# Attention and MLP mixer on one core: chunks of weights in the units' ring, and eight sums of weights moved into the first element's channel mixing

## The chip, the cores and the metric

The kernel runs on one core of a Trainium2 chip. The metric is the device time of one execution in microseconds (us). The core has five engines with a queue of instructions each, worked off in order: TensorE (PE; its weight loads are listed as PEld), VectorE (DVE), ScalarE (ACT), GpSimd (POOL) and the sync engine (SP), which here issues nearly all DMA transfers. An instruction that waits holds everything behind it in its queue. All data are float32, but the four weight matrices come as float64 and are converted to float32 by the kernel.

## The reference, cut to what matters

```python
# q, k, v: (8, 12, 448, 64); w_tok1 (448, 256), w_tok2 (256, 448), w_ch1 (768, 1536), w_ch2 (1536, 768)
q_n, k_n = rmsnorm(q, g_q), rmsnorm(k, g_k)
attn = softmax(q_n @ k_n.T / 8) @ v                  # per batch and head
x = attn.transpose(0, 2, 1, 3).reshape(8, 448, 768)
u = x + (relu(x.T @ w_tok1) @ w_tok2).T              # token mixing
out = u + relu(u @ w_ch1) @ w_ch2                    # channel mixing
```

## The kernel before, in words

**Batches.** The work goes over eight batches (elements) b, each with six pairs of head pairs in attention. Attention of batch b+1 runs beside the mixing of batch b: lists of small work items with a cost each are merged by `merge` in proportion to their costs, and `run` emits them in that order. This order is the order in which PE, DVE, ACT and POOL work; they are not reordered. The DMA issues of the sync queue are placed by a scheduler as they become ready in its own reckoning, so their order is seen in the built program.

**Mixing of one batch.** The attention result is held transposed, `uT` (768 rows in six tiles of 128, by 448). For token mixing it is turned: DVE transposes it into `xt` (L655, in the pool "tu", which has one buffer), four stores bring it to a DRAM scratch `xs` (L623), and a load brings it back as `x` (L630; the pool "x" has two buffers, one for each half). `tok1` (L669) and `tok2` (L677) are the two token products; DVE adds the second one to `uT` (L682). For batches 1 to 7 channel mixing uses seven products in place of eight (a Strassen form): the sums of activations go to "tu" (L698 to L701), `ch1` (L791) and `ch2` (L848) multiply by *units* of weights, 384 KB each, 42 per batch, which are loaded from a DRAM scratch `ws` by `load_units` (L724) into a ring of eight buffers (`unit_pool`). Four of the seven units of a group are plain blocks of the weights, or hold one; the rest are sums of the four blocks.

**Batch 0 prepares the weights.** Its channel mixing is done in the plain form, in 36 products of four matmuls each, one for every *chunk* of weights (`first_stage`, L765; L773 adds the second layer's result to `uT`). The 36 chunks (four blocks of 128 by 128, 512 KB in float64 and 256 KB in float32; w_ch1 is chunks 0 to 17, w_ch2 chunks 18 to 35) are loaded by two transfers each (`weight_load`, L177, five buffers in `raw_pool`), converted by bit operations (L248, L249, L251 and L266 on DVE, L259 on ACT) and written as a *stage* (L293 on DVE, `convert_last`), which PE multiplies by and which is also stored to `ws` (L193). Where a stage lies is told by `stage_home`: chunks 8 to 12 and 21, 22 in a tile of the pool "tu", chunks 13 and 14 in the pool "h1", the others in the ring of units, which no unit needs before batch 1. `weight_items` is the pipeline: item i loads chunk i+2, begins the conversion of chunk i, and ends that of chunk i-2. `first_items` places these items among the products: item k of the rest, which ends chunk 13+k, goes behind product `begins(k)`.

**Sums.** The seven-product form needs four sums of the four blocks of each chunk. `make` computes them on POOL in four instructions (L205 to L208), `send` stores them (L212). For the last six chunks (`direct`) they are made from the stage while it is still there. For the other 30 (`one`) the four blocks are loaded back from `ws` (L228) into a buffer of `raw_pool`, summed and stored; each of these steps lies one or more items behind the one before. The first three of these items run in the tail of batch 0, the next 25 in batch 1's token mixing and L791 part, the last five beside batch 1's L848 part. A unit that holds a sum can't be loaded before the sums of its group of chunks are sent (`has`): groups 0, 1, 2 are chunks 0 to 5, 6 to 11, 12 to 17; group 3 is 18 to 23, group 4 is 24 to 35.

**Output.** DVE turns each of the six output tiles of a batch (`trans_y`, L884, four buffers in `turn_pool`) and four stores send it (L613). The first four tiles of batch b are turned in the tail of batch b and sent in the token mixing of batch b+1; the last two are turned there, in buffers that the first two must have left.

Of the kernel before, what the change touches and what calls it, by code (L numbers as in the profile page):

```python
# [8 lines left out]
F32 = mybir.dt.float32  # L9
# [13 lines left out]
NQ = 8  # L23
# [21 lines left out]
def whole(ctx, tc, shifted, pre, q, k, v, g_q, g_k, moe_w_tok1, moe_w_tok2, moe_w_ch1, moe_w_ch2, out):  # L45


    nc = tc.nc
# [149 lines left out]
    def sum_items():  # L198
# [11 lines left out]
        def send(i):  # L210
            st["summed"].add(i)
            nc.sync.dma_start(out=slots(i, 4, 8), in_=eight(st.pop(("sum", i)))[:, 4:8])  # L212

        def direct(i):

            if i < n:
                st["sum", i] = raw_tile()
                make(st["stage", i], eight(st["sum", i]))
            if i > n - 6:
                send(i - 1)  # L220


        order = [*range(n - 18), *range(n - 12, n - 6), *range(n - 18, n - 12)]

        def one(i):
            if i < len(order):
# [7 lines left out]
                load_units(st["at"])  # L234

        def eight(t):
            return t[:].rearrange("p n w -> p (n w)").bitcast(F32).rearrange("p (q n) -> p q n", q=NQ)
        return ([(1.0, lambda i=i: direct(i)) for i in range(n - 6, n + 1)],
                [(1.0, lambda i=i: one(i)) for i in range(len(order) + 3)])

    def convert_first(i):
# [27 lines left out]
    def stage_home(j):  # L269


        if j in (8, 21):
            st["stages"] = tu_pool.tile([P, 4, KC, HS], F32, name="stages", tag="tu")
        if 8 <= j < 13 or 21 <= j < 23:
            o = (j - 8) % 13 * 4 * P
            return st["stages"][:].rearrange("p a b n -> p (a b n)")[:, o:o + 4 * P]
        if 13 <= j < 15:
            return h1_pool.tile([P, C], F32, name="stage", tag="h1")[:, 0:4 * P]
        t = unit_pool.tile([P, 3, 2, P], F32, name="stage", tag="unit")
        return t[:].rearrange("p t i n -> p (t i n)")[:, 0:4 * P]  # L280
# [351 lines left out]
            in_=st.pop("xs")[:].rearrange("(g p) n -> p g n", p=R))  # L632

    def x_tile(b, half):
        st["x", b, half] = x_pool.tile([P, KC, NS, P], F32, name="x")
        return st["x", b, half]

    def trans_x(b, j):
# [284 lines left out]

        return b < B - 1 and not shifted

    def first_items(tok, prods):


        convert = weight_items(BEFORE, len(chunks) + 3)
        items = merge(tok, convert[:5])  # L930
        n = len(stages) - 13
        for j, it in enumerate(prods[:-6]):
            items.append(it)
            items += [(0.0, convert[5 + k][1]) for k in range(len(convert) - 5) if begins(k, n) == j]
        return items, prods[-6:]

    def begins(k, n):

        return 2 + -(-k * 27 // (n - 1)) if k < n else 29

    def last_items(b):

# [45 lines left out]
    for part in pre.roots(2, st):  # L988
# [5 lines left out]

    run(merge(
        att_items(0, 8) + merge(att_items(8, AHEAD * per + 1), x_items(0, 0)), weight_items(0, BEFORE)))
    left, (direct, sums) = [], sum_items()
    for b in range(B):
        early, double = middle_items(b)
        if b == 0:  # L1000
            early, last = first_items(x_items(0, 1) + tok1_items(0, 0) + tok1_items(0, 1) + early, double)
        else:
            if in_next(b - 1):

                y, z = sends(b - 1, y_order(b - 1)[:4]), left
                left = [y[0], y[1], z[0], y[2], z[1], y[3]]
            run(merge(tok1_items(b, 0), left[:2]))
            begin, early = merge(tok1_items(b, 1) + early[:3 * KC], left[2:]), early[3 * KC:]
            if b == 1:
                early, double = merge(begin + early, sums[3:28]), merge(double, sums[28:])  # L1010
                begin = []
            early = begin + early + double
            early, last = early[:-4], early[-4:]
# [3 lines left out]
            att = att_items(lo, lo + 10) + x_items(b + AHEAD, 0) + att_items(lo + 10, lo + per)  # L1017
        if b == 0:
            last = x_items(1, 1) + merge(
                last, direct + sums[:3], turns(b, y_order(b)[:4], not in_next(b)))  # L1020
        else:
            if b + 1 < B:
                last = merge(last, x_items(b + 1, 1))
# [258 lines left out]
```

## Time and profile before

Median of 3 runs: 1362.38 us (1361.84 to 1365.18). The profiled execution: span 1360.3 us.

| engine | busy us | share | instructions |
|---|---|---|---|
| PE | 1290.7 | 95% | 7408 |
| PEld | 929.5 | 68% | 7408 |
| DVE | 748.0 | 55% | 1295 |
| ACT | 365.4 | 27% | 734 |
| POOL | 375.4 | 28% | 443 |

The stretches of the batches, cut at the first L669 of each:

| stretch, us | length | PE busy | POOL busy | DMA share |
|---|---|---|---|---|
| 92.60 to 272.70 (batch 0) | 180.10 | 172.33 | 32.45 | 0.60 |
| 272.70 to 452.45 (batch 1) | 179.75 | 163.66 | 102.58 | 0.93 |
| 452.45 to 610.00 (batch 2) | 157.55 | 154.70 | 40.01 | 0.67 |
| 610.00 to 767.60 (batch 3) | 157.60 | 154.73 | 40.03 | 0.68 |

How to read the views: a timeline line has the start and the length of a run of equal instructions, the engine, the line of the kernel, the operation with its output and inputs, and in brackets the idle time of the engine just before and what ended it. A busy PE is not a PE at full rate: after a stop its matmuls take longer. The DMA share is the mean busy share of the core's 16 DMA engines. The chain of work that ended last gives PE 78% of the span, DVE 10%, DMA 5%.

### The profile page before, as it was taken

Reading aid. Unit: us, or ns where it says so; the run is one execution under the profiler, and the core shown is the slowest. Engines: PE = TensorE matmul, PEld = TensorE weight load, DVE = VectorE, ACT = ScalarE, POOL = GpSimd, SP = SyncE. Lnnn points to the kernel's source line nnn. Section 1 sums busy time; section 2 is a strip of 40 time slices with the busy share of each in tenths; the row PEclk is TensorE's granted clock in tenths of the full one; section 3 lists DMA queues with packets and bytes.
Section 4 is the critical chain, followed back from the end, with each engine's and each line's share of the span. In section 5 each row is a group of like instructions: output and inputs, shape, how many; then the busy total and the mean of one; then the engine's idle time right before and its main releaser. Section 6 shows DMA issues by size and latency. Waiting matters only on the chain.

```text
span 1360.3 us, 20152 instructions
## 1 busy us (share of the span) xinstructions
PE 1290.7 (95%) x7408; PEld 929.5 (68%) x7408; DVE 748.0 (55%) x1295; ACT 365.4 (27%) x734; POOL 375.4 (28%) x443
## 2 busy tenths in 40 slices
PE   5989997998988999999999999999999999999997
PEld 3444443446777667794778757795777967787996
DVE  6878698563653366545556265644656365543212
ACT  5553442122320232303341123302322023300100
POOL 1211210366772231312231123312323133311220
PEclk9999998998999999999999999999999999999999
DMA  9655387689999666595568854595665956476654
GB/s 209 163 167 134 99 224 172 141 206 234 281 231 219 152 161 150 128 252 104 143 157 173 197 128 129 137 236 114 172 155 127 247 108 166 120 177 136 184 169 96
DMA packets 501520, 227.82 MB, mean 167 GB/s; under 512 B 373604, under 2 KB 463076, under 8 KB 501412
## 3 DMA queue, kind: packets, MB, share of 16 engines
q1 hardware_dynamic: 488290, 224.60, 67.1%
q10 hardware_dynamic: 12994, 1.84, 0.8%
q8 instruction: 61, 1.00, 0.3%
q14 instruction: 47, 0.39, 0.1%
q0 software_dynamic: 128, 0.00, 0.0%
HBM read 186.84 MB, written 39.52 MB: 166 GB/s over the span
## 4 chain that ended last, share of the span: by engine, by line
PE 78%; DVE 10%; DMA 5%; ACT 2%; issue 2%; SPq 1%; POOL 1%; DVEq 0%; ACTq 0%; POOLq 0%
PE m_ps L848 24%; PE m_ps L791 19%; PE m_ps L765 8%; PE o_ps L443 8%; PE s_ps L369 7%; PE m_ps L669 6%; PE m_ps L677 3%; DVE es L411 2%; DVE qk_t L334 2%; DMA unit<-ws 2%; PE d_ps L423 1%; DMA v<-in_v_dram 1%; ACT e L373 1%; PE m_ps L423 1%; DVE qkT L349 1%
## 5 line engine op out<-in xcount | busy, mean ns | idle before, releaser
L848 PE MATMUL m_ps<-hb,unit 128*128 128x224 f32 x1764 | 341.5, 355 | 7.7 <-DMA unit<-ws 5.8
L848 PEld LDWEIGHTS m_ps<-hb,unit 128*128 128x128 f32 x1764 | 333.2, 191 | 22.6 <-issue 13.0
L791 PE MATMUL m_ps<-tu,unit 128*128 128x224 f32 x1008 | 204.4, 358 | 3.0 <-DVE r L796 3.0
L791 PEld LDWEIGHTS m_ps<-tu,unit 128*128 128x128 f32 x1008 | 190.1, 192 | 22.4 <-DVE r L796 5.1
L373 ACT ACTIVATE e<-s_ps 128x448 f32<-128x448 f32 x336 | 157.0, 548 | 105.5 <-PE s_ps L369 104.8
L791 PE MATMUL m_ps<-uT,unit 128*128 128x224 f32 x756 | 154.7, 357 | 5.6 <-ACT r L812 3.1
L443 PE MATMUL o_ps<-e,v 64*64 64x448 f32 x1316 | 153.7, 543 | 4.6 <-DMA v<-in_v_dram 4.5
L791 PEld LDWEIGHTS m_ps<-uT,unit 128*128 128x128 f32 x756 | 140.6, 190 | 21.9 <-DVE uT L682 6.0
L369 PE MATMUL s_ps<-qkT 64*64 64x448 f32 x1260 | 145.7, 547 | 1.4 <-ACT qkT L352 1.4
L857 POOL TENSOR_TENSOR uT<-uT,r 128x448 f32<-128x448 f32 (+1 forms) x56 | 51.9, 937 | 265.1 <-DVE r L857 148.7
L796 DVE TENSOR_TENSOR r<-m_ps,r 128x448 f32<-128x448 f32 x63 | 38.9, 618 | 122.4 <-PE m_ps L791 69.8
L443 PEld LDWEIGHTS o_ps<-e,v 64*64 64x64 f32 x1316 | 50.6, 133 | 76.8 <-issue 70.7
L411 DVE TENSOR_TENSOR es<-es,e 128x896 f32<-128x896 f32 x84 | 94.2, 1122 | 14.9 <-ACT e L373 11.7
L857 DVE TENSOR_TENSOR uT<-uT,m_ps 128x448 f32<-128x448 f32 (+1 forms) x70 | 34.0, 502 | 122.5 <-PE m_ps L848 122.5
L369 PEld LDWEIGHTS s_ps<-qkT 64*64 64x64 f32 x1260 | 44.1, 132 | 71.7 <-issue 60.3
L411 POOL TENSOR_TENSOR es<-e 128x896 f32<-128x896 f32 x21 | 43.9, 2088 | 160.1 <-ACT e L373 160.1
L796 POOL TENSOR_TENSOR hb<-r,r 128x448 f32<-128x448 f32 x21 | 27.9, 1326 | 216.1 <-ACT r L812 166.8
L669 PE MATMUL m_ps<-x,w_sb 112*128 112x384 f32 x256 | 87.2, 494 | 0.0
L677 PE MATMUL m_ps<-w_sb,h 128*128 128x448 f32 x192 | 77.8, 549 | 6.3 <-DVE uT L682 6.3
L352 ACT ACTIVATE qkT<-qkT,g_t 128x448 f32<-128x448 f32 x36 | 24.1, 668 | 216.2 <-DVE qkT L349 216.2
L1164 DVE TENSOR_REDUCE ms<-sq 128x28 f32<-128x896 f32 (+2 forms) x45 | 48.8, 1084 | 59.5 <-ACT sq L1150 56.7
L669 PEld LDWEIGHTS m_ps<-x,w_sb 112*128 112x128 f32 x256 | 48.6, 193 | 36.4 <-ACT e L373 4.2
(114 smaller groups left out, 1357.3 us busy)
## 6 DMA issues: line engine op xcount, KB each, us to landing
unit<-ws SPq DMA_DIRECT2D x294, 384.0 KB, 4.1
raw<-in_moe_w_ch_dram SPq DMA_DIRECT2D x72, 256.0 KB, 3.5
v<-in_v_dram SPq DMA_DIRECT2D x94, 112.0 KB, 4.2
xs<-xt SPq DMA_DIRECT2D x56, 168.0 KB, 4.5
x<-xs SPq DMA_DIRECT2D x14, 672.0 KB, 7.3
out_dram<-turned SPq DMA_DIRECT2D x168, 56.0 KB, 2.0
ws<-raw SPq DMA_DIRECT2D x36, 256.0 KB, 4.4
qk_t<-in_q_dram SPq DMA_DIRECT2D x144, 56.0 KB, 3.0
```

Of the source, the lines that this page charges most:

```text
L369: nc.tensor.matmul(out=pss[i][rows_of(i, a), 0:S], lhsT=qkT[h, 1, k * D:(k + 1) * D], rhs=qkT[h, 0, :], start=True, stop=True)
L373: nc.scalar.activation(out=e[:, i, :], in_=pss[i][:, 0:S], func=AF.Exp)
L411: eng.tensor_tensor(out=es[:], in0=(es if k > 1 else st["e", t, 0])[:], in1=st["e", t, k][:], op=ALU.add)
L443: nc.tensor.matmul(out=st["o", p][a * D:(a + 1) * D, 0:S], lhsT=vt[rows, k * D:(k + 1) * D], rhs=e[rows, :], **kw)
L669: nc.tensor.matmul(out=ps[:, 0:HC], lhsT=w1_sb[0:R, c, jc * P:(jc + 1) * P], rhs=st["x", b, h][0:R, :, c, :], start=(c == 0), stop=(c == N ...
L677: nc.tensor.matmul(out=ps[:, 0:S], lhsT=st["h1", jc][:, cc * P:(cc + 1) * P], rhs=w2_sb[:, jc].rearrange("p c r -> p (c r)"), start=(jc == ...
L765: nc.tensor.matmul(out=ps, lhsT=a[:, o + 2 * half, :], rhs=natural(half)[:, :, t, :] if wide else u[:, half * KC + t, :], start=(t == 0 an ...
L791: nc.tensor.matmul(out=ps[:, j * HS:(j + 1) * HS], lhsT=w[:, t, j, :], rhs=m, start=(t == 0), stop=(t == KC - 1))
L796: add = lambda e, o, x, y: e.tensor_tensor(out=o, in0=x, in1=y, op=ALU.add)
L848: nc.tensor.matmul(out=ps[:, j * HS:(j + 1) * HS], lhsT=st["w"](j, t), rhs=hb[:, HB[what], t, :], start=(t == 0), stop=(t == KF - 1))
L857: add = lambda e, o, x, y: e.tensor_tensor(out=o, in0=x, in1=y, op=ALU.add)
L1164: self.nc.vector.tensor_reduce(out=st["ms", p][:, p % 2, lo:hi], in_=sq[:, lo:hi], axis=AX_X, op=ALU.add)
```

## The change

It has three parts. (1) `stage_home`: chunks 21 and 22 no longer lie in a tile of "tu" but in the ring of units like their neighbours. (2) `begins`: the places of the conversions among the products of batch 0 become 2, 4, 5, 7, 8, 9, 11, 12, 14, 15 and then 17 to 29 one by one, instead of 27 products divided evenly, so that a chunk takes a place of the ring after the chunk eight before it is used. (3) `sum_items`: the sums of chunks 0 to 7 are taken out of the list that runs in batch 1 and become ten items `some`, placed behind every second product of batch 0's channel mixing. They use tiles named `few` in the two buffers of the pool "x", which are free between batch 0's `tok1` and the load of batch 1's first half of `x`. The list `sums` is then 25 items instead of 33; five of them run in the tail of batch 0, fifteen in batch 1's token mixing and L791 part, five beside its L848 part. The purpose is to take transfers and POOL work from batch 1 into batch 0, and to take the wait for "tu" away.

```diff
+        FEW = 8
+
+        def some(i):
+            if 2 <= i:
+                send(i - 2)
+            if i < FEW:
+                t = st["sum", i] = x_pool.tile([P, KC, NS, P], F32, name="few", tag="x")
+                nc.sync.dma_start(out=eight(t)[:, 0:4], in_=slots(i, 0, 4))
+            if 1 <= i <= FEW:
+                q = eight(st["sum", i - 1])
+                make(q, q)
...
-        order = [*range(n - 18), *range(n - 12, n - 6), *range(n - 18, n - 12)]
+        order = [*range(FEW, n - 18), *range(n - 12, n - 6), *range(n - 18, n - 12)]
...
-        return ([(1.0, lambda i=i: direct(i)) for i in range(n - 6, n + 1)],
+        return ([(0.0, lambda i=i: some(i)) for i in range(FEW + 2)],
+                [(1.0, lambda i=i: direct(i)) for i in range(n - 6, n + 1)],
                 [(1.0, lambda i=i: one(i)) for i in range(len(order) + 3)])
...
-        if j in (8, 21):
+        if j == 8:
             st["stages"] = tu_pool.tile([P, 4, KC, HS], F32, name="stages", tag="tu")
-        if 8 <= j < 13 or 21 <= j < 23:
-            o = (j - 8) % 13 * 4 * P
+        if 8 <= j < 13:
+            o = (j - 8) * 4 * P
...
-            items += [(0.0, convert[5 + k][1]) for k in range(len(convert) - 5) if begins(k, n) == j]
+            items += [(0.0, convert[5 + k][1]) for k in range(len(convert) - 5) if begins(k) == j]
+            if j % 2 and j < 2 * len(some):
+                items.append(some[j // 2])
...
-    def begins(k, n):
-
-        return 2 + -(-k * 27 // (n - 1)) if k < n else 29
+    def begins(k):
+
+
+        return 2 + -(-k * 14 // 10) if k < 10 else min(k + 7, 29)
...
-                early, double = merge(begin + early, sums[3:28]), merge(double, sums[28:])
+                early, double = merge(begin + early, sums[5:20]), merge(double, sums[20:])
...
-                last, direct + sums[:3], turns(b, y_order(b)[:4], not in_next(b)))
+                last, direct + sums[:5], turns(b, y_order(b)[:4], not in_next(b)))
```

## The prediction

> **What bounds the kernel now.** I read the page first: TensorE (PE) is busy for 1290.7 of 1360.3 us, so only stretches in which PE stands can be won. The second view is the busy time of every engine per stretch; I cut it where the batch's first token matmul (L669) starts. The pieces of batch 1 and of batch 2 (token mixing; seven-product part L791; part L848) stand below one another.
>
> ```profile
> core 0: us, PE busy (x) PEld busy (x) DVE busy (x) ACT busy (x) POOL busy (x), PEclk, DMA share, GB/s
> 272.70:303.25 30.55, 28.69 (x146) 13.23 (x145) 17.87 (x31) 9.74 (x22) 20.53 (x30) 1.00 0.86 204
> 303.25:389.62 86.37, 77.91 (x461) 57.05 (x459) 40.81 (x69) 24.64 (x51) 59.80 (x95) 0.96 0.98 255
> 402.50:452.45 49.95, 44.18 (x237) 40.55 (x236) 18.64 (x33) 4.22 (x8) 13.50 (x20) 0.97 0.95 220
> 452.45:482.10 29.65, 28.70 (x145) 13.07 (x143) 15.20 (x31) 9.56 (x22) 7.49 (x6) 1.00 0.51 104
> 482.10:555.40 73.30, 71.40 (x461) 54.33 (x460) 41.41 (x74) 25.75 (x54) 23.04 (x18) 1.00 0.63 160
> 555.40:610.00 54.60, 54.60 (x321) 49.96 (x318) 28.98 (x49) 6.46 (x12) 9.48 (x10) 1.00 0.81 195
> ```
>
> Batch 1 does the same matmuls as batch 2 and takes 179.75 us against 157.55: 30.55, 86.37 and 62.83 us (389.62 to 452.45) against 29.65, 73.30 and 54.60. Its DMA share of 0.98 in the L791 part says why: the sums of the weights are read and written back there. The same view gives batch 0 180.10 us (92.6 to 272.7), with one hole. The timelines of VectorE (DVE) and PE show it:
>
> ```profile
> 217.28 0.64 DVE L349 STREAM_TRANSPOSE qkT<-qk_t 128x448 f32<-128x448 f32 x1
> 221.06 1.70 DVE L655 STREAM_TRANSPOSE xt<-uT 128x448 f32<-128x448 f32 x3 [3.14 <-PE m_ps L765]
> ...
> 230.55 1.15 DVE L773 TENSOR_TENSOR uT<-uT,m_ps 128x448 f32<-128x448 f32 x2
> ```
> ```profile
> 231.22 8.06 PE L765 MATMUL m_ps<-hb,stage 128*128 128x448 f32 x16 [7.19 <-DVE uT L773]
> ```
>
> DVE waits 3.14 us for the one "tu" place, held by chunks 21 and 22 until PE has used them; two conversions and two sums stand ahead of L773, for which PE waits. Last, the start of batch 1, DVE and then the sync queue:
>
> ```profile
> 284.24 0.65 DVE L884 STREAM_TRANSPOSE turned<-uT 128x448 f32<-128x448 f32 x1 [10.87 <-DMA out_dram<-turned]
> ...
> 291.16 0.61 DVE L682 TENSOR_TENSOR uT<-uT,m_ps 128x448 f32<-128x448 f32 x1
> ```
> ```profile
> 270.55 0.49 SPq L630 DMA_DIRECT2D x<-xs  x1
> 271.09 4.09 SPq L228 DMA_DIRECT2D raw<-ws  x3
> 275.23 1.81 SPq L724 DMA_DIRECT2D unit<-ws  x2
> 277.13 6.58 SPq L613 DMA_DIRECT2D out_dram<-turned  x8
> ...
> 308.45 2.25 SPq L724 DMA_DIRECT2D unit<-ws  x5
> ```
>
> DVE stands until the first output tile's four stores have landed (284.2), and the evacuation that token mixing needs (L682) follows 7 us later, at 291.16: just in time, since PE finishes the second product near 291.9.
>
> **The Trainium skill.** (1) "DMA: Bandwidth & Descriptors", Anatomy of one DMA: a DMA's semaphore wait sits on the issuing sequencer, before dispatch. So one waiting issue holds every later one of that queue. (2) The same page, Queues, rings and completion order: each DMA engine consumes descriptors in ring order. The trace agrees: the store issued from 277.13 on landed at 284.2, behind x, three raw loads and two units. (3) "TensorE: Matmul & The Clock Gate", Part 1: after an idle window of about 3.4 us PE is at half clock for as long. The trace agrees: behind the 7.19 us hole, 16 matmul records take 8.06 us, and at the rate of 24 in 9.22 us (chain, from 128.06) they would take 6.15: 1.9 us more. (4) "GPSIMD Engine Reference", 1. Specifications: GpSimd's (POOL) SBUF interfaces are shared with DVE. The trace agrees: a DVE L251 took 2.18 us at 195.38, beside a POOL sum, against a median of 0.43.
>
> **The change, part by part.**
>
> *Chunks 21 and 22 leave "tu".* No instruction is added. L655 need not wait: 3.14 us of DVE. They take two unit places, so each later chunk needs the place of the chunk eight before it; it is converted at product s-6, after s-8 is used. No wait of note.
>
> *Conversions later.* In the built order of the changed kernel one conversion fewer stands before L773: 2.86 us of DVE (five instructions: 0.69, 0.43, 0.69, 0.43, 0.69, overlapping a little). With the wait gone L773 would come 6.0 us earlier, at 224.5, and PE, done at 224.0, would hardly stand.
>
> *Eight sums beside batch 0's channel mixing.* Each adds a 256 KB load, four POOL subtractions and additions (4 x 0.456 us, the median of L205, = 1.83) and a 256 KB store. POOL has room: it is idle for 34.45 us before the sum at 192.63 and 41.25 us before 238.54. The added wait is on the sync queue: only two x places exist, so the load of sum i waits for the landed store of sum i-2, and the store waits for POOL. In the changed order the loads and stores go in pairs, one chunk's raw load between pairs. With 3.4 to 4 us from issue to landing (medians from 128 to 200 us: 3.3 for raw loads, 3.6 for stage stores) I walk the queue: stores 2, 3 at 160 and 162; loads 4, 5 at 164 and 165.5; raw load at 166 (before 163.5); stores 170, 171.6; loads 173.5, 175.3; raw load 175.7 (before 166.3); store 6 at 179.5, then the q/k loads (before from 173.3), and the raw loads at 181.6, 187.4 and 191.9 instead of 171.4, 179.4 and 183.0. What is queued behind is the raw loads, and DVE's conversions wait for them: landing takes 4 us, so conversions 8 and 9 would stand until 186 and 192, about 7 us of DVE idle in a stretch that was 92% busy (36.80 of 40 us, 160 to 200). DVE has about 6 us less to do by then, as conversions moved. Carrying the remaining work (18 us) from 209.7, I get L773 at 227.7, between 224.5 (nothing waits) and 234 (each landing 1.5 us longer, as the DMA share rises from 0.60 by 8 x 1.92 us in 72 us, the price below, to 0.81). I take 2 us saved in batch 0 (from -4 to +7).
>
> *Fewer sums in batch 1.* In the built order the L791 part has 13 sum loads and 13 stores instead of 20 and 20. Their price: (0.98 x 86.4 - 0.63 x 73.3) / 20 = 1.92 us of DMA time a pair. Seven less is 13.4 us; five unit loads also leave for the start, at some 1.5 us each. Demand falls from 84.6 to about 63.5 us, below batch 2's PE length of 73.3. The waits there (2.96 and 1.53 us for v, 1.44 for qkT, and the lost clock) go nearly all: I take 75.5 us, 11 saved (8 to 13). In the L848 part the last sums' stores still gate the last units, at the same matmul as before:
>
> ```profile
> 439.22 13.27 PE L848 MATMUL m_ps<-hb,unit 128*128 128x224 f32 x60 [4.20 <-DMA unit<-ws]
> ```
>
> So this wait stays and only the smaller one (1.57 us at 422) and some clock go: 3 saved (0 to 6).
>
> *The start of batch 1 pays.* Group 0 is summed already, so all seven units may load at once, and two more sums start. The built sync queue reads: x, four raw loads, a store that waits for POOL, a raw load, a second such store, seven units, and only then the first output stores. Before there were three raw loads and two units. POOL can't make the first sum before 279.1 (raw landing then) to 280.9, so the second store goes at 282.8 and the units from 283.3. Seven units are 2.75 MB; at 255 to 340 GB/s (slices of the DMA view here) 8 to 11 us. The first output tile lands at 294 to 297 instead of 284.2. DVE waits at L884 for it; behind it are the row norms and L682, 7 us later: 302. PE, which has done two products by 292.3, stands some 10 us, where before it stood 1.9 (L677), and loses 1.7 of clock: 10 us dearer (3 to 14).
>
> Sum: 1362.4 - 2 + 10 - 11 - 3 = 1356.4; I say 1356.
>
> **Rivals.** *The whole gain:* the output stores are not late, because the raw loads land sooner in an emptier queue and units go at the peak rate. Then the start costs nothing, batch 0 gives 6, L791 10, L848 3: 1343. For it: 0.58 DMA share from 240 to 272.7; against: the place of the stores behind seven units. *Slower:* DVE starves for raw weights and L773 comes 4 us later, the start costs 14, L791 gives 8, L848 2: 1370. For it: DVE at 92% with nothing to spare, one queue for everything, and POOL's added 14.6 us on the shared interface; against: later conversions leave slack. *Moved, not gained:* the batch-1 saving is given back whole at its start: 1362; this is the upper edge of the first case.
>
> **How the numbers follow.** First case 0.5, whole gain 0.25, slower 0.25. The first case spreads by some 5 us: faster than 1358.3 for 0.32 of its 0.5, the same for most of the rest. Faster 0.25 + 0.32 = 0.57, same 0.18, slower 0.25. The range 1345 to 1368 leaves out the outer part of both rivals, two in ten.
>
> **What would show it.** After: no wait before L655; PE's hole near 221 shorter; DMA share of the L791 part well below 0.98 and its length near 75; a DVE wait at L884 ending more than 8 us after where it ended before, with a PE hole in L677 behind it; the unit wait near the end of batch 1 still there. I am wrong if L884 ends as before (then 1343), if DVE shows waits for raw loads that sum to well over 7 us (then 1370), or if L791 stays above 80.

## The result, and the profile after

The changed kernel takes 1353.08 us (median of 4 runs, 1352.70 to 1355.33) against 1362.11 us before (median of 4, 1359.00 to 1365.18): a ratio of 0.9937, with a 95% interval of 0.9912 to 0.9962. The forecast was 1356 us, in a range of 1345 to 1368, with faster as the likeliest. The total is 3 us from the forecast, but this is in part luck: batch 0 came out 3.8 us dearer than its term, and the two product parts of batch 1 together 4.9 us cheaper than theirs.

The profiled execution has a span of 1351.2 us. First its busy time per stretch, cut as before: batch 0, then token mixing, the part of the seven products (now L807, before L791) and the second part (now L864, before L848) of batch 1. Line numbers have grown: by 13 at the loads of the sums (now L241), by 16 to 18 below them.

```profile
core 0: us, PE busy (x) PEld busy (x) DVE busy (x) ACT busy (x) POOL busy (x), PEclk, DMA share, GB/s
92.60:274.43 181.83, 172.33 (x739) 81.11 (x738) 141.68 (x220) 57.70 (x106) 55.26 (x86) 0.98 0.69 176
274.43:313.45 39.02, 30.91 (x146) 13.85 (x144) 15.75 (x31) 9.47 (x22) 20.06 (x30) 0.91 0.87 216
313.45:384.59 71.14, 68.75 (x430) 53.27 (x429) 42.11 (x66) 23.46 (x46) 42.85 (x61) 1.00 0.91 229
384.59:443.71 59.12, 58.00 (x349) 50.72 (x349) 32.56 (x57) 9.13 (x20) 21.62 (x31) 1.00 0.88 224
```

Batch 0 is 1.7 us longer than before (181.83 against 180.10), token mixing of batch 1 is 8.5 longer (39.02 against 30.55), the two product parts together are 18.9 shorter (130.26 against 149.20). From batch 2 on nothing has changed: 907.49 us to the end, before 907.85. The sum, 1.7 + 8.5 - 18.9 - 0.4 = -9.1, is the difference of the two spans.

One trap lies in the third and fourth row. The counts in brackets show 430 PE records where there were 461, and 349 where there were 317. The groups by line name them: 16 score and 16 output matmuls of attention (L385, L459) have slid from the third row into the fourth, because the shorter list of sums changed how the items are merged. Sixteen of each take 1.74 and 1.68 us. With like work the parts are 74.6 and 55.7 us, before 86.4 and 62.8 (good to a few tenths, since the records of neighbouring matmuls overlap).

The timeline of DVE, the lines that answer those shown of before:

```profile
186.87 0.43 DVE L264 TENSOR_SCALAR e_t<-raw 128x512 uint32<-128x512 uint32 x1 [1.21 <-DMA raw<-in_moe_w_ch_dram]
192.89 0.43 DVE L264 TENSOR_SCALAR e_t<-raw 128x512 uint32<-128x512 uint32 x1 [3.19 <-DMA raw<-in_moe_w_ch_dram]
230.96 1.14 DVE L789 TENSOR_TENSOR uT<-uT,m_ps 128x448 f32<-128x448 f32 x2
241.93 0.43 DVE L264 TENSOR_SCALAR e_t<-raw 128x512 uint32<-128x512 uint32 x1 [2.46 <-DMA raw<-in_moe_w_ch_dram]
296.14 0.65 DVE L900 STREAM_TRANSPOSE turned<-uT 128x448 f32<-128x448 f32 x1 [20.89 <-DMA out_dram<-turned]
```

The wait for "tu" is gone (L671, before L655, runs at 221.5 without one). In its place stand waits for raw weights of 1.21, 3.19 and 2.46 us, and L789 (before L773) comes at 230.96, no earlier than the 230.55 of before. The wait at L900 (before L884) has doubled. The timeline of PE shows what these cost:

```profile
231.63 7.83 PE L781 MATMUL m_ps<-hb,stage 128*128 128x448 f32 x16 [7.52 <-DVE uT L789]
256.28 18.31 PE L781 MATMUL m_ps<-hb,stage 128*128 128x448 f32 x48 [1.43 <-DVE uT L789]
299.36 6.59 PE L693 MATMUL m_ps<-w_sb,h 128*128 128x448 f32 x12 [7.14 <-ACT h L688]
432.29 11.59 PE L864 MATMUL m_ps<-hb,unit 128*128 128x224 f32 x60 [1.12 <-DMA unit<-ws]
```

The first hole is as long as before, the second (256) and the third (299, in token mixing) are new or grown, and the wait for units near batch 1's end has shrunk from 4.20 to 1.12 us. The third hole names ACT L688, not DVE: that activation is queued on ACT behind a step of the row norms (L1190) which waits for DVE, and DVE stands at L900:

```profile
297.78 1.01 ACT L1190 COPY half<-ms 32x56 f32<-32x56 f32 x4 [11.80 <-DVE ms L1182]
298.82 0.49 ACT L688 ACTIVATE h<-m_ps 128x384 f32<-128x384 f32 x1
```

Last the sync queue at the start of batch 1:

```profile
272.38 5.47 SPq L241 DMA_DIRECT2D raw<-ws  x4
282.07 0.36 SPq L212 DMA_DIRECT2D ws<-raw  x1
282.48 0.51 SPq L241 DMA_DIRECT2D raw<-ws  x1
283.85 0.36 SPq L212 DMA_DIRECT2D ws<-raw  x1
284.30 3.47 SPq L740 DMA_DIRECT2D unit<-ws  x7
287.86 7.73 SPq L629 DMA_DIRECT2D out_dram<-turned  x8
```

Two stores that wait for POOL's sums, then seven units, then the output stores, as the forecast walked it.

### The profile page after: what moved, and what is told of

It reads as the page before. It is cut to its first block, busy times and chain, and to the rows that moved or that the text cites. A ratio compares the mean times of both kernels' runs of the same rounds, so it can differ in the third digit from the quotient of the medians.

```text
span 1351.2 us, 20151 instructions
## 1 busy us (share of the span) xinstructions
PE 1284.4 (95%) x7408; PEld 925.0 (68%) x7408; DVE 753.5 (56%) x1295; ACT 366.2 (27%) x734; POOL 380.4 (28%) x443
## 4 chain that ended last, share of the span: by engine, by line
PE 76%; DVE 11%; DMA 5%; SPq 2%; ACT 2%; POOL 2%; issue 2%; DVEq 0%; ACTq 0%; POOLq 0%
PE m_ps L864 25%; PE m_ps L807 19%; PE o_ps L459 8%; PE s_ps L385 8%; PE m_ps L781 7%; PE m_ps L685 5%; PE m_ps L693 3%; DVE es L427 2%; DVE qk_t L350 2%; DMA unit<-ws 2%; PE d_ps L439 1%; ACT e L389 1%; DVE uT L698 1%; DVE qkT L365 1%; PE m_ps L439 1%
## 5 line engine op out<-in xcount | busy, mean ns | idle before, releaser
L864 PEld LDWEIGHTS m_ps<-hb,unit 128*128 128x128 f32 x1764 | 332.1, 190 | 14.8 <-issue 11.3
L864 PE MATMUL m_ps<-hb,unit 128*128 128x224 f32 x1764 | 339.5, 354 | 1.1 <-DMA unit<-ws 1.1
L807 PE MATMUL m_ps<-tu,unit 128*128 128x224 f32 x1008 | 202.8, 356 | 3.9 <-DVE r L812 3.8
L807 PEld LDWEIGHTS m_ps<-tu,unit 128*128 128x128 f32 x1008 | 188.3, 190 | 23.0 <-DVE r L812 6.2
L807 PE MATMUL m_ps<-uT,unit 128*128 128x224 f32 x756 | 155.0, 357 | 6.3 <-ACT r L828 3.1
L807 PEld LDWEIGHTS m_ps<-uT,unit 128*128 128x128 f32 x756 | 140.4, 190 | 23.2 <-DVE uT L698 7.0
L459 PE MATMUL o_ps<-e,v 64*64 64x448 f32 x1316 | 149.4, 541 | 0.1
L385 PE MATMUL s_ps<-qkT 64*64 64x448 f32 x1260 | 145.1, 547 | 0.2 <-ACT qkT L368 0.2
L812 DVE TENSOR_TENSOR r<-m_ps,r 128x448 f32<-128x448 f32 x63 | 39.0, 619 | 124.1 <-PE m_ps L807 64.5
L459 PEld LDWEIGHTS o_ps<-e,v 64*64 64x64 f32 x1316 | 49.7, 133 | 69.7 <-issue 64.9
L812 POOL TENSOR_TENSOR hb<-r,r 128x448 f32<-128x448 f32 x21 | 27.9, 1326 | 239.6 <-ACT r L828 181.3
L385 PEld LDWEIGHTS s_ps<-qkT 64*64 64x64 f32 x1260 | 44.0, 132 | 70.0 <-issue 60.6
L693 PEld LDWEIGHTS m_ps<-w_sb,h 128*128 128x128 f32 x192 | 35.5, 194 | 53.8 <-issue 24.4
```

The lines of the kernel that those rows point to most:

```text
L385: nc.tensor.matmul(out=pss[i][rows_of(i, a), 0:S], lhsT=qkT[h, 1, k * D:(k + 1) * D], rhs=qkT[h, 0, :], start=True, stop=True)
L459: nc.tensor.matmul(out=st["o", p][a * D:(a + 1) * D, 0:S], lhsT=vt[rows, k * D:(k + 1) * D], rhs=e[rows, :], **kw)
L693: nc.tensor.matmul(out=ps[:, 0:S], lhsT=st["h1", jc][:, cc * P:(cc + 1) * P], rhs=w2_sb[:, jc].rearrange("p c r -> p (c r)"), start=(jc == ...
L807: nc.tensor.matmul(out=ps[:, j * HS:(j + 1) * HS], lhsT=w[:, t, j, :], rhs=m, start=(t == 0), stop=(t == KC - 1))
L812: add = lambda e, o, x, y: e.tensor_tensor(out=o, in0=x, in1=y, op=ALU.add)
L864: nc.tensor.matmul(out=ps[:, j * HS:(j + 1) * HS], lhsT=st["w"](j, t), rhs=hb[:, HB[what], t, :], start=(t == 0), stop=(t == KF - 1))
```

## The experiments

All of them, with the changed kernel for comparison. "Products" is the time from batch 0's first product to batch 1's first token matmul, "hole" PE's first hole in it, for L773 or L789, "start" is batch 1's token mixing, "parts" the two product parts of batch 1 together; these four are read from the PE timeline of each kernel's profiled execution (it puts before's first token matmul of batch 1 at 272.55, 0.15 us ahead of the cut used above). The time and the ratio to the kernel before are from all its runs, "profiled" is the time of the profiled execution.

| kernel | us | ratio, 95% interval | profiled | products | hole | start | parts |
|---|---|---|---|---|---|---|---|
| before | 1362.11 | | 1362.08 | 144.55 | 7.19 | 30.70 | 149.08 |
| changed | 1353.08 | 0.9912 to 0.9962 | 1352.96 | 146.35 | 7.52 | 39.02 | 130.26 |
| places | 1361.61 | 0.9981 to 1.0006 | 1367.18 | 145.12 | 6.08 | 32.39 | 150.79 |
| home_only | 1361.17 | 0.9984 to 1.0000 | 1359.30 | 142.71 | 5.41 | 30.70 | 148.17 |
| sums_only | 1354.32 | 0.9930 to 0.9960 | 1354.60 | 147.02 | 8.54 | 39.21 | 129.83 |
| no_make | 1354.17 | 0.9920 to 0.9964 | 1355.70 | 149.56 | 6.04 | 38.79 | 130.87 |
| late_conv | 1353.72 | 0.9923 to 0.9950 | 1355.65 | 147.16 | 4.72 | 39.15 | 130.64 |
| few12 | 1354.63 | 0.9925 to 0.9954 | 1354.27 | 151.13 | 9.28 | 36.85 | 127.49 |
| y_first | 1350.31 | 0.9899 to 0.9928 | 1351.40 | 147.21 | 7.75 | 32.06 | 133.29 |
| best | 1350.62 | 0.9890 to 0.9922 | 1353.70 | 154.02 | 5.42 | 32.25 | 129.26 |
| stores_begins | 1352.87 | 0.9930 to 0.9957 | 1350.20 | 147.83 | 10.18 | 34.78 | 131.31 |
| stores_tail3 | 1350.92 | 0.9914 to 0.9942 | 1347.17 | 147.12 | 9.03 | 31.43 | 132.74 |
| y_act | 1360.79 | 0.9982 to 1.0006 | 1362.21 | 146.03 | 7.50 | 48.14 | 128.99 |
| y_tail3 | 1347.77 | 0.9880 to 0.9921 | 1355.12 | 147.37 | 9.13 | 32.02 | 137.34 |

The profiled execution is not always near the median: that of places is 5.6 us above it and that of y_tail3 7.4, both among the slowest of their kernels, as is best's; those of stores_begins and stores_tail3 are the fastest of theirs. Differences of 1 or 2 us in the last four columns are no more than hints.

### First question: why did batch 0 gain nothing?

**places.** The first two parts of the change alone, on the kernel before:

```diff
-        if j in (8, 21):
+        if j == 8:
...
-        if 8 <= j < 13 or 21 <= j < 23:
-            o = (j - 8) % 13 * 4 * P
+        if 8 <= j < 13:
+            o = (j - 8) * 4 * P
...
-        return 2 + -(-k * 27 // (n - 1)) if k < n else 29
+        return 2 + -(-k * 14 // 10) if k < 10 else min(k + 7, 29)
```

> The kernel before with the places and the conversions of the change, but with all sums of weights where they were (none beside batch 0's channel mixing). Theory (the step of the prediction taken alone: DVE's 3.14 us wait for the tu place and one conversion of 2.86 us leave the stretch ahead of the token-mixing evacuation, and the eight added sums ate both): the evacuation L789 comes at 224 to 226, PE's hole of 7.2 us there shrinks below 2.5 us, batch 1 begins at 264 to 267 instead of 272.7, and the total is 1354 to 1356. Rival (the hole is set by when the raw weights land, not by the wait: DVE just waits elsewhere): L789 at 229 to 231, batch 1 begins at 271 to 273, total 1361 to 1363.

Measured: 1361.61 us, no difference that can be told, and L773 at 230.92. The first product of this execution starts at 129.48, in before at 128.00, and from there PE needs 96.03 us to the hole in both (and in the changed kernel), so the length of the hole tells more than the time of L773:

```profile
231.59 9.32 PE L765 MATMUL m_ps<-hb,stage 128*128 128x448 f32 x16 [6.08 <-DVE uT L773]
```

The hole is 1.1 us shorter than before, where 4.7 and more were expected, and the 16 matmuls behind it take 1.3 us longer than before's 8.06. My theory fell: even without the sums the places give little in the hole and nothing in the total. The timeline of DVE of this kernel shows where the freed time went:

```profile
190.33 0.69 DVE L266 SCALAR_TENSOR_TENSOR raw<-raw,e_t 128x512 uint32<-128x512 uint32 x1 [3.22 <-ACT e_t L259]
...
202.80 0.72 DVE L266 SCALAR_TENSOR_TENSOR raw<-raw,e_t 128x512 uint32<-128x512 uint32 x1 [2.05 <-ACT e_t L259]
...
230.92 1.15 DVE L773 TENSOR_TENSOR uT<-uT,m_ps 128x448 f32<-128x448 f32 x2
```

DVE waits for ACT's step of the conversion (L259). The timeline of ACT says why that step is late:

```profile
187.64 0.54 ACT L775 ACTIVATE hb<-m_ps 128x448 f32<-128x448 f32 x1 [5.75 <-PE m_ps L765]
189.15 0.54 ACT L775 ACTIVATE hb<-m_ps 128x448 f32<-128x448 f32 x1 [0.96 <-PE m_ps L765]
189.59 0.71 ACT L259 ACTIVATE e_t<-e_t,expo_c 128x512 uint32<-128x512 uint32 x1
```

ACT does its steps in order, and L259 is queued behind the evacuation of a finished product (L775), which waits for PE. So DVE can't run ahead of PE: through ACT it is held to PE's place in the products. Fewer conversions ahead of that place make DVE arrive early and wait; in the main only DVE's work behind the last such point moves L773. Counted from the last row-norm step (L1181, which all these kernels reach) the dependence is plain:

| kernel | DVE at the row norm | conversions from there to L773 | other wait there | L773 | difference |
|---|---|---|---|---|---|
| before | 209.15 | 3 | 3.14 (tu) | 230.55 | 21.40 |
| places | 210.05 | 4 | none | 230.92 | 20.87 |
| changed | 210.10 | 4 | none | 230.96 | 20.86 |

A conversion is 2.86 us of DVE. The new begins put one more conversion behind the row norm (they took two from ahead of it), and this eats the 3.14 us of the wait but for 0.5 us. All the kernels agree: with three conversions and no wait this stretch takes 18.13 to 18.15 us (five kernels), with four 20.86 to 20.88 (six); only few12 and best, with more sums in batch 0, need longer. DVE's arrival at the row norm is less fixed than the table makes it look: counted from the first product it is 81.2, 80.6 and 82.0 us in the three kernels, so the eight sums did cost 1.4 us ahead of it, and the hole went from 6.08 to 7.52. Two further kernels test the count of conversions.

**home_only.** On the kernel before, the edit of `stage_home` shown above and no other: the wait should go, and no conversion come in its place.

> The kernel before with one edit: chunks 21 and 22 get unit places; conversions begin when they did, sums stay where they were. Theory (DVE and PE are brought into step around product 20, because the ScalarE part of a conversion is queued behind the evacuation of a PE result; only DVE's work and waits after that, from about 200 us on, set L773. The change freed the 3.1 us tu wait there but put one more conversion of 2.86 us behind the step, so places alone gave nothing): now the wait goes and no conversion is added behind the step, L773 comes at 227 to 228.5 instead of 230.55, PE's hole shrinks from 7.2 to about 4, batch 1 begins at 268.5 to 270, total 1358 to 1359. Rival (PE's hole is set by something else, the arrival of raw weights): as with the places and the conversions together, L773 at 230 to 231, total 1361 to 1362.

```profile
205.84 0.69 DVE L293 SCALAR_TENSOR_TENSOR stage<-raw 128x512 f32<-128x512 f32 x1 [1.39 <-PE m_ps L765]
...
228.93 1.15 DVE L773 TENSOR_TENSOR uT<-uT,m_ps 128x448 f32<-128x448 f32 x2
```

Measured: from the row norm (210.80) to L773 18.13 us, the predicted 18 of three conversions without a wait. But a new wait of 1.39 us stands ahead of it, for a place in the ring that PE has not left, so L773 is 1.6 us earlier and not 2 to 3.5, and PE's hole is 5.41 us. In the profile batch 0's products are 1.8 us shorter; the times give a ratio of 0.9992 (0.9984 to 1.0000), a gain of some 1 us that can't quite be told from nothing. The expected total of 1358 to 1359 was not met.

**late_conv.** The changed kernel with one conversion moved behind L789:

```diff
-        return 2 + -(-k * 14 // 10) if k < 10 else min(k + 7, 29)
+        return 2 + -(-k * 14 // 10) if k < 10 else min(k + 7 + (k > 13), 29)
```

> The changed kernel with the conversions from the fifteenth on begun one product later, so that one conversion fewer (2.86 us of DVE) stands between the step and L789; nothing else. Theory: L789 comes at 228 to 228.5 instead of 231.0, PE's hole is 4.5 to 5 instead of 7.5, and since later products have their stages in time, batch 1 begins 2 to 3 us earlier, total 1350 to 1351. Rival (DVE is short in all of batch 0's second half, so the conversion is missed later): the hole is shorter, but PE then waits at the next evacuation or for a stage by as much, total 1352.5 to 1354.

```profile
229.45 7.76 PE L781 MATMUL m_ps<-hb,stage 128*128 128x448 f32 x16 [4.72 <-DVE uT L789]
256.02 20.00 PE L781 MATMUL m_ps<-hb,stage 128*128 128x448 f32 x48 [3.42 <-DVE uT L789]
```

Measured: row norm at 210.63, L789 at 228.78, 18.15 us, so three conversions again; the first hole falls by 2.8 us. But the second, at 256, grows by 2.0 and the 48 matmuls behind it take 20.00 us instead of 18.31; the total, 1353.72 us, is that of the changed kernel. Theory right on the hole, rival right on the total: DVE has this conversion to do before the next evacuation as well, and there it waits for raw weights too (2.73 us at 240.0).

**sums_only.** The changed kernel with `stage_home` and `begins` of before, so only the third part.

> The changed kernel with the places and the conversion order of the kernel before: only the eight sums are moved into batch 0. Theory (the two parts add up: the sums cost batch 0 some 7 us through DVE, the places give 6): the tu wait of about 3 us is back, the evacuation L789 comes at 236 to 239, batch 1 begins at 279 to 282, batch 1 is as long as in the changed kernel (169 us), total 1358 to 1361. Rival (the places give nothing; batch 0 is set by the DMA and the raw weights): batch 1 begins at 273 to 276, total 1352 to 1355.

Measured: 1354.32 us, batch 1 from 275.75 on: the rival's figures. The total can't be told from the changed kernel's, so the eight sums alone give the gain, and the first two parts of the change give none that these runs can tell. They don't add up as the theory had it. With early conversions DVE reaches the row norm only at 214.49, behind waits for raw weights of 3.0 us, and needs 18.14 us from there; with the late ones it is there at 210.10 and needs 20.86. Counted from the first product L789 comes 1.0 us later, and that much longer is the hole (8.54 against 7.52).

**no_make.** The changed kernel without POOL's arithmetic for the eight moved sums; loads and stores stay.

```diff
-                q = eight(st["sum", i - 1])
-                make(q, q)
+                pass
```

> The changed kernel without the arithmetic of the eight moved sums (no GpSimd instruction for them; each store writes the loaded half back, so these weights are wrong); their loads and stores stay, 256 KB each. Theory (in batch 0 it is GpSimd's share of the SBUF port that slows DVE): the DVE instructions between 165 and 215 us are back at their usual 0.43 and 0.69 us, L789 comes at 224 to 227 instead of 231.0, PE's hole of 7.5 us shrinks to 0.5 to 3, batch 1 begins at 267 to 270, total 1346 to 1349. Rival (the late raw loads behind the sums' loads and stores on the one queue do it): DVE's waits for raw stay or only move by the 2 us of a sum, L789 stays at 229 to 231, total 1351 to 1353.

They stay, but not in their places. With no sum to wait for, the sync queue issues all eight loads and eight stores between 105.6 and 145.3 us; in the changed kernel they reach to 205.5. So this edit takes POOL's work and the transfers out of the stretch ahead of L789 together (its DMA share is 0.60, in the changed kernel 0.73), and it can't decide between theory and rival.

Measured: 1354.17 us, above both ranges. The hole is 6.04 us, that of places (6.08), and DVE's waits are those of places too: for ACT 0.47, 3.22 and 2.04 us ahead of L789, for raw weights none there, and 2.54 at 243.6 (places 0.47, 3.22, 2.05, none, 2.67 at 242.1). So the last of the three waits for raw weights comes with the new begins, and the first two with the sums. Next the groups by line of the same stretch (from the L350 at 158 us, in this kernel at 161, to L789), first of the changed kernel, then of this one:

```profile
L309 DVE SCALAR_TENSOR_TENSOR stage<-raw 128x512 f32<-128x512 f32 x13 | 9.9, 764 | 0.0
L264 DVE TENSOR_SCALAR e_t<-raw 128x512 uint32<-128x512 uint32 x13 | 6.0, 459 | 4.8 <-DMA raw<-in_moe_w_ch_dram 4.4
```
```profile
L282 DVE SCALAR_TENSOR_TENSOR raw<-raw,e_t 128x512 uint32<-128x512 uint32 x13 | 10.7, 827 | 5.7 <-ACT e_t L275 5.7
L309 DVE SCALAR_TENSOR_TENSOR stage<-raw 128x512 f32<-128x512 f32 x13 | 8.9, 686 | 0.0
```

POOL does slow DVE. One L309 takes 764 ns in the mean beside the sums and 686 without; in the timeline of the changed kernel it takes 0.94 us at 164.63 and 174.01, while POOL makes sums, and 0.69 at 181.53, while POOL is idle. (Not every mean compares so: in each kernel two DVE instructions near 195 us meet a wide softmax sum of POOL and take 2.2 to 2.6 us, but they are of other lines, here one of L282's, which lifts its mean to 827.) In all DVE is busy 65.06 us in that stretch against 61.17: 3.9 us dearer, which agrees with what the Trainium skill says in "GPSIMD Engine Reference", 1. Specifications, that GpSimd's SBUF interfaces are shared with DVE. Yet the stretch is only 1.4 us longer (72.59 against 71.19), because without the sums DVE waits 5.7 us for ACT, where with them it waits 4.4 for raw weights. Both costs lie ahead of the point where DVE is held to PE, and there they replace that wait but for these 1.4 us; which of the two costs the 1.4, this kernel doesn't tell.

The total says little here: PE waits 1.33 us for v at 139.5, among the transfers that came forward, and is slower around it, so that it reaches its hole 4.6 us later after the first product than in the changed kernel. Without that the products would take 145.0 us and not 149.56.

### Second question: what is the price at batch 1's start?

**y_first.** The changed kernel with two units at the end of batch 0, the other five once batch 1 has begun:

```diff
-                load_units(st["at"])
+                load_units(st["at"] if i > 4 else 3 - UNITS)
...
-            load_units(0)
+            load_units(3 - UNITS)
```

> The changed kernel, but until batch 1 has begun only two of the seven units are loaded; the other five follow on the queue behind the first eight output stores. Theory (the output stores behind seven units are what makes batch 1's start long): DVE's wait at L900 ends at 286 to 289 instead of 296.1, L698 is done by 294, PE's hole of 7.1 us in L693 falls below 2, the first phase of batch 1 takes 31 to 33 us instead of 39.0, total 1345 to 1347. Rival (the DMA engines are the bound through batch 1's first phases, with shares of 0.87 and 0.91, so the five units are then missed later): the start is 6 us shorter, but PE waits for units or v in the L807 part by as much, total 1351 to 1353.

The sync queue, then DVE:

```profile
284.67 0.93 SPq L740 DMA_DIRECT2D unit<-ws  x2
285.69 5.54 SPq L629 DMA_DIRECT2D out_dram<-turned  x8
...
292.42 2.43 SPq L740 DMA_DIRECT2D unit<-ws  x5
```
```profile
291.32 0.65 DVE L900 STREAM_TRANSPOSE turned<-uT 128x448 f32<-128x448 f32 x1 [14.71 <-DMA out_dram<-turned]
```

Measured: 1350.31 us; its interval overlaps that of the changed kernel, but all six runs (1348.84 to 1351.40) lie below every run of the changed kernel and of sums_only. L900's wait ends 4.8 us earlier, later than the 286 to 289 expected (batch 1 begins 1.4 us later here, though), but this is enough: the start takes 32.06 us, 7.0 less, with no hole over 1 us. So the stores behind the units were the cause of the long start. But the parts take 3.0 us more. In this kernel DMA is busy for 0.89 of 32.06 and 0.97 of 74.40 us, together 100.7 us; in the changed kernel for 0.87 of 39.02 and 0.91 of 71.14, together 98.7. The transfers are the same but for two more loads of sums, the time for them is 3.7 us less, and PE now waits in the first part (1.87 us for DVE L812 at 346.3, behind row norms whose input from ACT, L1168, had kept DVE waiting for 4.91 us and had itself waited 7.05 us for a transfer). The rival was half right: the start gave 7, and 3 to 4 came back as a load on the DMA engines.

**y_act.** Batch 0's output stores on ACT's queue, all else as changed:

```diff
-            (nc.sync if in_next(b) else nc.scalar).dma_start(
+            (nc.sync if in_next(b) and b else nc.scalar).dma_start(
```

> The changed kernel with batch 0's output stores issued on ScalarE's queue instead of the sync queue; all else, the seven units too, as it was. Theory (it is the order on the one issuing queue that holds the stores): issued at 277 to 280, the first tile's stores share the DMA engines with four raw loads and then the units, L900's wait ends at 284 to 289 instead of 296.1, the hole in L693 goes, the first phase takes 31 to 34 us, total 1346 to 1351 (less what eight and more issues cost ScalarE, some 0.6 us each). Rival (the transfers themselves hold them, behind the raw loads and units on the same DMA engines): L900 ends at 293 to 296, the first phase takes 37 to 39 us, total 1352 to 1354.

```profile
281.74 0.65 DVE L900 STREAM_TRANSPOSE turned<-uT 128x448 f32<-128x448 f32 x1 [5.83 <-DMA out_dram<-turned]
```
```profile
289.03 5.45 PE L685 MATMUL m_ps<-x,w_sb 112*128 112x384 f32 x8 [8.62 <-DMA x<-xs]
```

Measured: 1360.79 us, worse than either theory said. L900's wait ends at 281.7, 14 us earlier: it was the place on the queue that held the stores. But the sync queue's waits of this kernel show 9.7 us of an L212 store for these output stores, which ACT issues only at 277.9, behind an activation that waits for PE. Behind that L212 stand x and everything else, so PE waits 8.62 us for x. Later ACT is held for 11.05 us by seven issues of output stores; they take 0.32 to 0.64 us each, and the rest is time between them. A new wait replaced the old one; why the sync queue's store had to wait for the stores of another queue, and what held ACT between its issues, the trace doesn't say.

### Third question: is batch 1 still bound by transfers?

**few12.** Twelve sums in batch 0 instead of eight (`FEW = 12`, and the slices of `sums` for batch 1 are 5 to 17 and from 17).

> The changed kernel with twelve instead of eight sums beside batch 0's channel mixing (the last at product 27); batch 1 has four fewer. Theory (transfers are still the bound in batch 1's L807 and L864 parts at shares of 0.91 and 0.88, four pairs are 7.7 us of DMA time there, while in batch 0 a sum costs DVE 0.2 us): the two parts take 128 to 129 us instead of 130.3, batch 0 ends 0.5 to 1 us later, total 1352 to 1353. Rival (the remaining 2.5 us over batch 2 is arithmetic on DVE and GpSimd, not transfers, and batch 0 pays more as its queue gets fuller after 200 us): parts stay at 130, batch 0 ends 2 to 4 us later, total 1355 to 1357.

Measured: the parts take 127.49 us, which is batch 2's 127.8: the theory's side. So the last 2.8 us over batch 2 go with the sums; whether with their transfers or with their arithmetic on POOL is not shown, since both left together. But batch 0's products are 4.8 us longer, more than the rival's 2 to 4. From the row norm to L789 it takes 22.46 us for four conversions, 1.6 more than without the late sums, the first hole is 9.28 us, the second 3.39. The total, 1354.63 us, is no better.

**best** puts y_first, late_conv and few12 together.

> Output stores ahead of five units, the conversions one product later, and twelve sums in batch 0, together. Theory (with the stores first, batch 1's start is 32 us, and the L807 part paid 3.3 us for it only because the transfers moved there; twelve sums make room there; the conversion gives 2 to 3): total 1344 to 1347. Rival (what the stores gained is bound by all transfers of batch 1 together and the conversion gives nothing): 1349 to 1351.

Measured: 1350.62 us, the rival's range and no better than y_first alone. The parts are 4.0 us shorter than in y_first, as the theory had it, but batch 0's products take 154.02 us: with late conversions and late sums DVE waits 6.44 us for raw weights at 244, and PE's second hole is 8.14 us.

### Toward a better version

**stores_begins** is y_first with the places and begins of before.

> The changed kernel with the first eight output stores ahead of five of the units, and with the kernel before's places and begins of conversions (chunks 21 and 22 in the tu place, conversions early). Theory (the new begins cost batch 0 as much behind the step as the freed wait gave, and bring DVE's wait for raw weights near 242 and PE's second hole near 256; the stores' order gives 2.8 us whatever batch 0 does): no second hole near 256, PE's first hole about 8.5 as in the kernel with the sums alone, batch 0 as long as there within 1 us, the first phase of batch 1 takes 32 us, total 1350 to 1352. Rival (the stores' gain depended on the new begins): 1353 to 1355.

Measured: 1352.87 us, between the two ranges and nearer the rival's. There is no second hole, but the first is 10.18 us: with early conversions the waits for raw weights (5.55 us) are no longer behind a wait for ACT, DVE is at the row norm at 214.25 and needs 18.14 us. The start takes 34.78 us with a hole of 2.93. Against sums_only the stores' order gives 1.5 us, which the intervals can't tell from nothing; with the late begins it gave 2.8. So the late begins seem to help where the stores go first (y_first is 2.6 us faster), though they gain nothing alone.

**stores_tail3** is stores_begins with `sums[:3]` instead of `sums[:5]` in the tail of batch 0.

> As the kernel with the stores ahead of five units and the conversions begun early, and only three instead of five of the later sums begun at the end of batch 0, so that no store that waits for a GpSimd sum stands ahead of the output stores. Theory (the rest of DVE's wait at L900, 14.7 us with the stores ahead, is those two stores): L900's wait ends 4 to 6 us earlier, about 10 us after DVE's last evacuation of batch 0 as in the kernel before, the first phase of batch 1 takes 30.5 to 31 us instead of 32, total 1349 to 1351. Rival (the two sums are only moved into the parts that transfers bind): the L807 and L864 parts grow by 1.5 to 3 us, total 1351 to 1354.

```profile
285.47 0.65 DVE L900 STREAM_TRANSPOSE turned<-uT 128x448 f32<-128x448 f32 x1 [10.80 <-DMA out_dram<-turned]
```

Measured: 1350.92 us. L900's wait is 10.80 us (stores_begins 16.65), as long as before the change (10.87), and the start takes 31.43 us: the rest of that wait came from what the two sums put ahead of the output stores, their loads and the two stores that wait for POOL. The parts grow by 1.4 us, just short of the rival's 1.5 to 3, and the total lies near the upper end of the theory's range.

**y_tail3**: the same edit on y_first, with the late begins.

> The changed kernel with its own places and begins, the output stores ahead of five units, and three later sums instead of five begun at the end of batch 0, so that nothing that waits for GpSimd stands ahead of the output stores. Theory (the two edits to the sync queue and the late begins each keep their worth: 2.8 us for the stores, some 2 for the two sums): the first phase of batch 1 takes 30.5 to 31.5 us, the two parts after it 133 to 134, total 1347.5 to 1349. Rival (the two sums just move into the parts that transfers bind): the two parts take 135 or more, total 1350 to 1352.

Measured: 1347.77 us, ratio 0.9901 (0.9880 to 0.9921): the lowest median of all, and in the expected range. From y_first (0.9899 to 0.9928) it can't be told apart for certain. Its profiled execution, the slowest of its six (1355.12 us; the others took 1344.78 to 1351.09), shows the wait at L900 shortened to 11.31 us, but not the phases expected: the start takes 32.02 us and not 30.5 to 31.5, and the parts 137.34, the rival's "135 or more", with before's wait for units near the end of batch 1 back:

```profile
430.63 14.32 PE L864 MATMUL m_ps<-hb,unit 128*128 128x224 f32 x60 [4.21 <-DMA unit<-ws]
```

Whether the faster executions do without that, the one profile can't say; so the theory is borne out in the total alone. In medians the two sums less at the end of batch 0 gave 2.0 us with the early begins and 2.5 with the late ones, and the late begins 2.6 and 3.2.

## Why the prediction was right, and where it was not

**Batch 0: -2 predicted, +1.8 measured** (products 144.55 to 146.35). The step that failed is "Carrying the remaining work (18 us) from 209.7, I get L773 at 227.7". Up to there the walk held: the three late raw loads were issued at 182.5, 188.9 and 193.8 (181.6, 187.4 and 191.9 predicted), DVE's waits for them ended at 186.9 and 192.9 (186 and 192) and summed to 4.4 us (7 predicted), POOL's 3.9 us were not in the sum at all, and DVE still came to the row norm at 210.1, because most of both lay where it would have waited for ACT. The remaining work was mis-sized: I had counted that one conversion fewer precedes L773 in all, and not that one *more* stands behind the row norm; it is 20.9 us and not 18, and L789 came at 231.0. home_only and late_conv, with three conversions there, gave 18.13 and 18.15 us. The other 1.4 us are the second hole at 256, behind a later wait for raw weights (2.46 us at 242) for which I had no term; it comes with the new begins, since places shows it without any sums (2.67 us) and sums_only doesn't. And "L655 need not wait: 3.14 us of DVE" was right as a fact and no gain.

**Start of batch 1: +10 predicted, +8.5 measured.** The mechanism and its times held: second store 283.85 (predicted 282.8), units from 284.3 (283.3), first tile landed at 296.1 (294 to 297), L698 at 301.4 (302). PE stood from 292.2 (292.3 predicted), but only to 299.4: the first thing that waited behind L900 was not L698 but the activation L688, so the hole was 7.1 us and not 10. y_first took 7.0 of this back by order alone, and paid 3.0 of them again in the parts behind.

**L791 part: -11 predicted.** With like work it went from 86.4 to 74.6, against a predicted 75.5. The demand worked out from the price of a pair, 63.5 us of DMA, was 0.91 x 71.14 = 64.7. The price was right, the count only nearly: 11 pairs and 21 units were issued in this part, not 13 and 19, and with these the same sum gives 62.8. That the share stayed at 0.91, and not well below 0.98, is because the same demand now fills a shorter time.

**L848 part: -3 predicted, -7 measured** with like work (62.8 to 55.7). The step that failed is "So this wait stays and only the smaller one (1.57 us at 422) and some clock go". I had taken the last units to be tied to the same matmul because their sums are. The last units are still issued 2.7 us after the last store of a sum (426.19 and 428.93; before 433.00 and 435.81). But that store went 41.6 us after its part began instead of 43.4, and PE reached the wait after 46.6 us instead of 45.4, now that 32 attention matmuls had moved into the part; so the wait fell from 4.20 to 1.12 us, some 1.8 of it by the earlier store and 1.2 because work that had moved in now fills the wait. The smaller one (1.57) and a wait of 1.91 for DVE at the start of the part went whole, and L848's 252 matmuls were busy 48.9 us instead of 50.9, without the slow ones behind such holes. That the store came earlier because the queue was less full is likely, not shown. Without the split by like work the two parts together gave 18.9 us, where 14 were forecast.

**The rivals.** "The whole gain" failed, since the output stores were late by the 12 us that the walk of the queue gave; "slower" and "moved, not gained" failed, since the start returned 8.5 of 18.9 us.

## What to carry to other kernels

An engine that is tied to another one, here DVE to PE by ACT's queue, has no single sum of work: find the last point where it is held, and count only what the change adds or removes behind that point. When prefetches are set free earlier, look at what was issued behind them: seven units that no one needed yet cost 7 us of the first phase by standing ahead of small stores that held back a buffer, and putting those first gave 2.8 us of the total. And when an experiment takes work away, look where the rest of it went: in no_make the transfers that were meant to stay had moved ahead by up to 60 us.

## What the runs showed of the hardware that was not expected

- A DVE instruction of 128x512 takes longer beside small POOL instructions (128x128, 0.46 us each when alone): in the changed kernel an L309 took 0.94 us at 164.63 and 0.69 at 181.53, an L264 0.57 at 172.06 and 0.43 at 182.85. Beside a wide one it takes up to five times as long: an L264 of 0.43 us took 2.31 us at 193.3 in few12, with a 128x896 instruction of 2.08 us on POOL from 193.25.
- What a stop costs PE does not follow from its length. The 16 matmuls behind the first hole of batch 0 took 7.76 to 9.32 us in these fourteen kernels, where 16 without a stop take 6.28 (at 139.71 in the changed kernel): 7.76 behind 4.72 us in late_conv, 9.32 behind 6.08 in places, 8.35 behind 10.18 in stores_begins.
